# Block-sparse attention and a two-layer FFN: neighbour keys loaded from DRAM instead of copied on chip, and one early load of V put behind the first gathers

## The chip, the cores and the metric

The kernel runs on one core of a Trainium2 chip. The metric is device time in microseconds (us); the profile's span runs from the core's first to its last instruction. Engines are named as the profile does: PE is TensorE (PEld its weight loads), DVE is VectorE, ACT is ScalarE, POOL is GpSimd, SP is SyncE, which here does nothing but issue DMAs.

## The reference

Four batches, eight heads, 768 positions, 64 values a head. Positions are cut into 24 blocks of 32. A query block sees the blocks beside it and itself, the first and the last block, and three sampled blocks; the first and last query block see everything. Behind the softmax and the product with V stands an FFN with softplus between its two matrices.

```python
mask = np.abs(blk_i - blk_j) <= window          # window = 1
mask = mask | (blk_i == 0) | (blk_j == 0) | (blk_i == n_blocks - 1) | (blk_j == n_blocks - 1)
for qb in range(n_blocks):
    for kb in sampled_blocks[qb]:
        mask[qb*block:(qb+1)*block, kb*block:(kb+1)*block] = True
scores = np.where(mask, scores, -1e9)           # then softmax, attn @ v
h = x @ w_in                                    # x: (3072, 512), w_in: (512, 2048)
g = np.maximum(h, 0.0) + np.log1p(np.exp(-np.abs(h)))
return g @ w_out                                # w_out: (2048, 512), float64 weights
```

## The kernel before, in words

**Attention in sets.** The 22 inner query blocks of each of 4 batches make 88 blocks, taken four at a time: 22 groups (`j` from 0 to 21), each one "s" set. A group can straddle two batches (22 is not a multiple of 4): groups 5 and 16 do. The first and last blocks of each batch make four "w" sets, which see all keys. For an "s" set, four query blocks each have eight key blocks: slots 0 to 2 hold the three neighbours, 3 and 7 the first and last block, 4 to 6 the sampled ones. They are laid side by side in one of two key buffers `kg`, which groups use in turn (`kd = kg[j % 2]`, line 504).

**Keys.** A batch's keys lie in SBUF in one tile `kT` (lines 451 to 457), loaded by SP; there is one buffer, so the next batch's load waits for the "w" set's scores, which are the last readers. `gather_keys` (line 503) makes the pieces of work that fill `kg`: `beside` (line 511) copies the three neighbours of all blocks of the group in one VectorE copy (line 515; ScalarE for group 0) and, where the batch changed, the two end blocks (line 524, ScalarE). `of_block` (line 531) copies the sampled blocks, three GpSimd copies a query block (line 544), the block number read from a register. The group's first `of_block` calls `beside`.

**Values.** `load_values` (line 553) fills one of two buffers `vbuf`: the rows of the near blocks in one SP DMA of 1 MB from a host-made array (line 568), the sampled rows by four indirect DMAs of GpSimd, 256 KB each (line 572). "w" sets load whole rows of V (line 563).

**A set's work.** `scores` (line 586; matmuls at 605, mask and minimum by VectorE at 611), `exponents` (ACT, 660), `transposes` (PE 673, copies out of PSUM at 676 and 678), `products` (PE 709), `normalise` (745), `turn` (771), then the high and low parts of x (784, 788). Line 629 holds the "w" sets' scores, 723 their products.

**Order.** SP runs in program order, POOL too in a few stretches; the other engines' order comes from a scheduler, except where an instruction is held in program order. `pieces` (line 795) lists the attention's pieces; `attend` (line 904) issues one, then takes one or two waiting key and value pieces (`gather`, line 481) and then steps of `convert`, the splitting of the float64 weights: raw loads by SP (line 178, four buffers, so each waits for VectorE to be done with an older one), ACT at 185 and 189, VectorE at 195 to 212, parking of later weights by SP (line 231). `scored` asks for the keys of group j + 2 once group j's scores are issued (line 809); `valued` asks for the values two sets ahead. In the program, line 513's work of group j + 2 so stands right behind the load of the queries of set m + 2 (line 468). From some 50 us on, attention is woven with the FFN's first part (hidden layer 263 to 265, projection 327 to 329); behind it the second part runs with PE alone in front (1113 to 1115, 1225 to 1227).

**The start.** SP issues, in this order: keys of batch 0 (line 454), queries of sets 0 and 1 (468), near rows of set 0 and of set 1 (568), queries of set 2 (468), three raw weight loads (178). POOL, in program order: the gathers of set 0 (572), the twelve key copies of group 1 (544):

```python
    load_values(0)
    ...
    with tc.manual_schedule(engines={mybir.EngineType.Pool}):
        gathered(value_work, 0)
        gathered(key_work, 1)
    load_values(1)
```

Of the kernel before, what the change touches and what calls it, by code (L numbers as in the profile page):

```python
# [19 lines left out]
BLOCK = 32  # L20
# [17 lines left out]
PARK = 8  # L38

WARM = 28  # L40

AHEAD = 0.5

# [11 lines left out]
def sparse_attention_ffn(  # L55
# [25 lines left out]
    nc = tc.nc  # L81
    NM, P, NP, NI, _ = q.shape
# [10 lines left out]
    NR = 3  # L93
# [293 lines left out]
    for rows in (slice(0, NR * BLOCK), slice(NR * BLOCK, P)):  # L387
        nc.gpsimd.iota(first[rows], pattern=[[0, 1]], base=0, channel_multiplier=1)
    vbuf = [ac.tile([P, 2, NI, DM], F32, name=f"vg{n}") for n in range(2)]

    nc.gpsimd.indirect_dma_start(
        out=vbuf[0][:, 0, 0, :], out_offset=None, in_=v,
# [55 lines left out]
    kT, qc, vg = {}, {}, {}  # L448
# [23 lines left out]
    def registers(eng, us):  # L472
        for u in us:
            if (eng, u) not in regs:
                regs[eng, u] = eng.value_load(pk32[0:1, u : u + 1], min_val=0, max_val=(1 << 31) - 1)
        return [regs[eng, u] for u in us]
# [9 lines left out]
    def gathered(work, m):  # L486
        while work and work[0][0] <= m:
            work.pop(0)[1]()
# [3 lines left out]
    def load_keys(*js):  # L492

        for j in js:
            if j < NM:
                of = [b for b, _ in group[j]]
                wanted.extend((j, b, of.index(b), of.index(b) + of.count(b)) for b in sorted(set(of)))
        while wanted and wanted[0][1] in kT and not waiting:
            gather_keys(*wanted.pop(0))
# [3 lines left out]
    def gather_keys(j, b, lo, hi):  # L503
        kd = kg[j % 2]
        blk0 = group[j][lo][1]

        stale = [i for i in range(lo, hi) if ended_in.get((j % 2, i)) != b]
        for i in stale:
            ended_in[j % 2, i] = b

        def beside():

            at = kT[b][:, blk0 - 1 : blk0 - 1 + NR, :]
            pattern = [list(x) for x in at.ap]
            ins = (nc.vector.tensor_copy if j else nc.scalar.copy)(
                out=kd[:, lo:hi, 0:NR, :].rearrange("p i s f -> p i (s f)"),
                in_=bass.AP(at.tensor, at.offset, [pattern[0], [NP * BLOCK, hi - lo], [1, NR * NP * BLOCK]]),
            )
            tc.keep_in_program_order(ins)
            if stale:  # L520
                rows = slice(stale[0], stale[-1] + 1)
                first = nc.vector.tensor_copy if j == 0 else nc.scalar.copy
                for end, slot, blkno in ((first, NR, 0), (nc.scalar.copy, 2 * NR + 1, LAST)):
                    ins = end(
                        out=kd[:, rows, slot, :],
                        in_=kT[b][:, blkno : blkno + 1, :].to_broadcast([P, len(stale), NP * BLOCK]),
                    )
                    if j or slot > NR:
                        tc.keep_in_program_order(ins)

        def of_block(i):

            eng = (nc.vector if i < 2 else nc.scalar) if j == 0 else nc.gpsimd
            copy = nc.scalar.copy if j == 0 and i >= 2 else eng.tensor_copy
            if i == lo and j:
                beside()
            blk = group[j][i][1] - 1
            (r,) = registers(eng, [blk // 2])
            for s in range(NR):
                x = nc.s_assert_within(  # L540
                    eng.snap((r >> (16 * (blk % 2) + 5 * s)) & 31), 0, LAST,
                    skip_runtime_bounds_check_because="a sampled block is one of the key blocks",
                )
                copy(  # L544
                    out=kd[:, i, 1 + NR + s, :], in_=kT[b][:, bass.ds(x, 1), :].rearrange("p n f -> p (n f)")
                )

        if j == 0:
            key_work.append((j, beside))
        key_work.extend((j, lambda i=i: of_block(i)) for i in range(lo, hi))  # L550


    def load_values(m):
        if m >= len(sets):
            return
        what, j = sets[m]
        vd = vg[sets[m]] = vbuf[m % 2]
        if what == "w":
            b = j
            rows = vd.rearrange("p c i f -> p (c i) f")  # L560
            for n in range(0, NCH, 2):
                lo = b * S + n * P
                nc.sync.dma_start(
                    out=rows[:, n : n + 2], in_=v[lo : lo + 2 * P].rearrange("(t p) f -> p t f", p=P)
                )
            return
        i0 = 1 if m == 0 else 0
        nc.sync.dma_start(out=vd[:, 0, i0:NI], in_=near[j, :, i0:NI])

        def of_block(i):  # L570
            b, blk_ = group[j][i]
            nc.gpsimd.indirect_dma_start(  # L572
                out=vd[:, 1, i, :],
                out_offset=None,
                in_=v,
                in_offset=bass.IndirectOffsetOnAxis(ap=ix[:, b, blk_ : blk_ + 1], axis=0),
            )

        value_work.extend((m, lambda i=i: of_block(i)) for i in range(NI))
# [288 lines left out]
    warm = ps_s.tile([P, 4, P], F32, tag="s", name="warm")  # L868
    for n in range(WARM):
        nc.tensor.matmul(warm[:, n % 4], ident, ident, start=True, stop=True)  # L870
# [12 lines left out]
    with tc.manual_schedule(engines={mybir.EngineType.Pool}):  # L883
        gathered(value_work, 0)
        gathered(key_work, 1)
    load_values(1)
    load_keys(2)
    scores(1)
# [577 lines left out]
```

## Time and profile before

| | us |
|---|---|
| median of 3 runs | 762.72 (761.26 to 763.01) |
| the profiled execution | 759.56 |
| its span | 757.8 |

| engine | busy us | share |
|---|---|---|
| ACT | 555.1 | 73% |
| POOL | 274.6 | 36% |

HBM reads are 105.97 MB and writes 30.41 MB. In the page's slices each digit is the tenth of a slice (18.9 us) in which an engine was busy. A row of the windows view gives, for one stretch, each engine's busy us (with the count of its instructions), the granted clock of PE, the busy share of the 16 DMA engines and what they moved. A row of the timeline gives start, duration, engine, line and tile, and in brackets how long the engine stood idle ahead of it and who ended that. The chain of waits gives start, duration and what.

### The profile page before, as it was taken

How to read it: one execution, taken by the hardware profiler on the slowest of the kernel's cores; microseconds unless marked ns; L12 is line 12 of the kernel's file. 1: busy time of each engine (PE TensorE's matmuls, PEld its weight loads, DVE VectorE, ACT ScalarE, POOL GpSimd, SP SyncE). 2: the span in 40 equal slices, each digit the busy share in tenths (PEclk: the TensorE clock that was granted, in tenths of full speed). 3: DMA queues.
4: the chain of work that ended last, by engine and by line, in shares of the span. 5: the costliest groups of instructions: out<-in, count | busy, mean ns of one | idle time of the engine just before them, and what ended most of it. 6: DMA issues, size and time to landing. Idle time of an engine off the chain costs nothing.

```text
span 757.8 us, 21892 instructions
## 1 busy us (share of the span) xinstructions
PE 726.4 (96%) x8324; PEld 618.0 (82%) x8324; DVE 587.7 (78%) x1445; ACT 555.1 (73%) x1298; POOL 274.6 (36%) x446
## 2 busy tenths in 40 slices
PE   7888899999999999999999989999999999999997
PEld 5557677878887787887889877899999999999995
DVE  5689999877888779886688775777676776766865
ACT  5679997877878788876678668766676566675663
POOL 7754535415454146540200259551515125020000
PEclk9899999999999999999999999999999999999999
DMA  8788875969658897667526261131133023300301
GB/s 330 259 314 336 336 256 190 348 221 382 244 181 329 281 358 266 229 252 240 196 106 240 100 209 51 62 112 56 58 112 112 25 87 112 106 8 1 112 1 56
DMA packets 54335, 137.79 MB, mean 182 GB/s; under 512 B 5781, under 2 KB 18582, under 8 KB 50518
## 3 DMA queue, kind: packets, MB, share of 16 engines
q1 hardware_dynamic: 46740, 112.40, 41.8%
q0 software_dynamic: 7120, 23.34, 8.3%
q8 instruction: 65, 1.06, 0.6%
q10 hardware_dynamic: 370, 0.66, 0.2%
q14 instruction: 40, 0.33, 0.1%
HBM read 105.97 MB, written 30.41 MB: 180 GB/s over the span
## 4 chain that ended last, share of the span: by engine, by line
PE 69%; ACT 12%; DVE 10%; DMA 4%; issue 3%; POOL 2%; SPq 1%; POOLq 0%; DVEq 0%; ACTq 0%
PE o L1225 7%; PE o L1226 7%; PE o L1227 7%; PE h L263 3%; PE t L673 3%; PE x L709 3%; PE a L1113 3%; PE a L1115 3%; PE a L1114 3%; ACT pr L660 3%; PE h L264 3%; PE h L265 3%; PE o L327 3%; PE o L328 3%; PE o L329 3%; PE s L605 3%
## 5 line engine op out<-in xcount | busy, mean ns | idle before, releaser
L572 POOL DMA_INDIRECT vg<-in_v_dram,ix x88 | 95.6, 1087 | 103.5 <-PE x L709 78.1
L660 ACT ACTIVATE pr<-pr,nmax 128x256 f32<-128x256 f32 (+1 forms) x192 | 102.0, 533 | 30.2 <-DVE nmax L611 20.2
L544 POOL COPY kg<-kT 128x128 f32 x252 | 73.7, 333 | 87.7 <-PE s L605 82.9
L1225 PE MATMUL o<-w,gh 128*128 128x512 f32 x240 | 94.3, 393 | 0.0
L1226 PE MATMUL o<-w,gh 128*128 128x512 f32 x240 | 94.2, 393 | 0.0
L1227 PE MATMUL o<-w,gl 128*128 128x512 f32 x240 | 94.0, 392 | 0.0
L1200 ACT CAST gh<-a 128x512 fp32r<-128x512 f32 x30 | 17.6, 587 | 79.1 <-DVE a L1196 79.1
L263 PE MATMUL h<-x,w 128*128 128x384 f32 x192 | 69.4, 361 | 2.9 <-ACT pt L678 1.3
L611 DVE CUSTOM_DVE_ANT_1 pr<-s,mask 128x256 f32<-128x256 f32 x176 | 62.9, 420 | 7.4 <-PE s L605 7.4
L265 PE MATMUL h<-x,w 128*128 128x384 f32 x192 | 64.8, 338 | 0.1
L264 PE MATMUL h<-x,w 128*128 128x384 f32 x192 | 64.8, 337 | 0.0
L673 PE MATMUL t<-ident,pr 128*128 128x128 f32 x448 | 61.3, 278 | 2.3 <-ACT pr L660 0.9
L709 PEld LDWEIGHTS x<-vg,pt 128*32 128x32 f32 x2816 | 42.1, 110 | 23.6 <-issue 17.7
L327 PE MATMUL o<-w,gh 128*128 128x512 f32 x144 | 58.8, 408 | 0.0
L673 PEld LDWEIGHTS t<-ident,pr 128*128 128x128 f32 x448 | 51.0, 142 | 8.7 <-ACT pr L660 3.5
L709 PE MATMUL x<-vg,pt 128*32 128x64 f32 x2816 | 48.2, 220 | 9.4 <-issue 6.1
L329 PE MATMUL o<-w,gl 128*128 128x512 f32 x144 | 57.1, 397 | 0.0
L328 PE MATMUL o<-w,gh 128*128 128x512 f32 x144 | 57.0, 396 | 0.0
L605 PE MATMUL s<-kg,qc 64*32 64x256 f32 x1408 | 52.2, 391 | 1.8 <-DVE u L276 1.4
L1227 PEld LDWEIGHTS o<-w,gl 128*128 128x128 f32 x240 | 45.1, 188 | 10.1
L1184 DVE SCALAR_TENSOR_TENSOR b<-b,e 128x512 f32<-128x512 f32 x30 | 20.9, 698 | 39.8 <-ACT l L1180 39.8
L678 ACT COPY pt<-t 128x512 f32<-128x512 f32 x82 | 45.8, 585 | 6.9 <-PE t L673 6.8
(207 smaller groups left out, 2147.5 us busy)
## 6 DMA issues: line engine op xcount, KB each, us to landing
vg<-in_near_dram SPq DMA_DIRECT2D x21, 1024.0 KB, 5.7
xD<-x SPq DMA_DIRECT2D x8, 1536.0 KB, 12.7
raw<-in_w_in_dram SPq DMA_DIRECT2D x16, 512.0 KB, 9.0
raw<-in_w_out_dram SPq DMA_DIRECT2D x16, 512.0 KB, 6.8
q<-xD SPq DMA_DIRECT2D x16, 512.0 KB, 7.0
vg<-in_v_dram SPq DMA_DIRECT2D x12, 512.0 KB, 4.5
yD<-os SPq DMA_DIRECT2D x24, 256.0 KB, 3.2
y<-yD SPq DMA_DIRECT2D x24, 256.0 KB, 3.5
```

What stands on the lines that cost most here:

```text
L263: nc.tensor.matmul(out_, wh[:, cols], hi, start=(c == 0), stop=False)
L264: nc.tensor.matmul(out_, wh[:, cols], lo, start=False, stop=False)
L265: nc.tensor.matmul(out_, wl[:, cols], hi, start=False, stop=(c == NC - 1))
L327: nc.tensor.matmul(po[m], gh[:, cols], wh, start=first, stop=False)
L329: nc.tensor.matmul(po[m], gl[:, cols], wh, start=False, stop=last)
L572: nc.gpsimd.indirect_dma_start(out=vd[:, 1, i, :], out_offset=None, in_=v, in_offset=bass.IndirectOffsetOnAxis(ap=ix[:, b, blk_ : blk_ + 1 ...
L660: nc.scalar.activation(x, x, AF.Exp, bias=nmax[:, r, j : j + 1], scale=-1.0, accum_out=rs[:, h : h + 1])
L673: nc.tensor.transpose(ps[:, i], st["pr"][r][:, c * P : (c + 1) * P], ident)
L709: nc.tensor.matmul(xq[rows, h * D : (h + 1) * D], pt[r, 2 * j + c][:, rows], vd[:, c, i, h * D : (h + 1) * D], start=(c == 0), stop=(c == 1),)
L1225: nc.tensor.matmul(po[m], gh[:, cols], wh, start=first, stop=False)
L1226: nc.tensor.matmul(po[m], gh[:, cols], wl, start=False, stop=False)
L1227: nc.tensor.matmul(po[m], gl[:, cols], wh, start=False, stop=last)
```

## The change

From group 4 on (`LOADED = 4`), the three neighbours' keys of a group come in one SP DMA straight from the keys in DRAM, `k[b]`, into `kg`, in place of the VectorE copy out of `kT`. The groups 1 to 3 keep the copy. Shapes and destination are the same: for each partition and query block one run of 3 x 128 float32. The DMA is no longer held in program order with VectorE; SP's own order is the program's. Second, POOL clears one element a partition of `vbuf[1]`'s first near row behind the gathers of set 0 and the key copies of group 1; the near load of set 1 writes over it and so waits for it.

```diff
+LOADED = 4
...
         def beside():
-            at = kT[b][:, blk0 - 1 : blk0 - 1 + NR, :]
+            at = (kT[b] if j < LOADED else k[b])[:, blk0 - 1 : blk0 - 1 + NR, :]
             pattern = [list(x) for x in at.ap]
-            ins = (nc.vector.tensor_copy if j else nc.scalar.copy)(
-                out=kd[:, lo:hi, 0:NR, :].rearrange("p i s f -> p i (s f)"),
-                in_=bass.AP(at.tensor, at.offset, [pattern[0], [NP * BLOCK, hi - lo], [1, NR * NP * BLOCK]]),
-            )
-            tc.keep_in_program_order(ins)
+            out_ = kd[:, lo:hi, 0:NR, :].rearrange("p i s f -> p i (s f)")
+            in_ = bass.AP(at.tensor, at.offset, [pattern[0], [NP * BLOCK, hi - lo], [1, NR * NP * BLOCK]])
+            if j < LOADED:
+                tc.keep_in_program_order((nc.vector.tensor_copy if j else nc.scalar.copy)(out=out_, in_=in_))
+            else:
+                nc.sync.dma_start(out=out_, in_=in_)
...
         gathered(value_work, 0)
         gathered(key_work, 1)
+        nc.gpsimd.memset(vbuf[1][:, 0, 0, 0:1], 0.0)
     load_values(1)
```

## The prediction

> **What bounds the kernel now.** I read the page's busy shares and slices first, then the windows by stage, then the chain and the timeline of the places the change touches.
>
> ```profile
> PE 726.4 (96%) x8324; PEld 618.0 (82%) x8324; DVE 587.7 (78%) x1445; ACT 555.1 (73%) x1298; POOL 274.6 (36%) x446
> ...
> PE   7888899999999999999999989999999999999997
> ...
> DMA  8788875969658897667526261131133023300301
> ```
>
> PE is busy 96% of the span. The holes are in the first five or six slices (0 to 114 us); that is also where the DMA engines are fullest. The windows say what is full there:
>
> ```profile
> 30.00:66.00 36.00, 29.20 (x626) 20.38 (x627) 32.73 (x98) 29.15 (x75) 20.57 (x34) 1.00 0.84 305
> 66.00:124.00 58.00, 53.46 (x933) 42.30 (x932) 57.25 (x158) 53.09 (x142) 33.06 (x69) 1.00 0.82 306
> 124.00:335.00 211.00, 207.04 (x3403) 173.09 (x3403) 175.64 (x495) 173.17 (x450) 93.76 (x193) 1.00 0.75 272
> ```
>
> From 66 to 124 us VectorE is busy 57.25 of 58 us: it is the bound there, ScalarE (53.09) and PE (53.46) next. From 124 us PE is busy 207.04 of 211 us and VectorE only 83%: VectorE time is worth little there. The first 26 us are bound by something else:
>
> ```profile
> 18.07 0.30 PE L709 MATMUL x<-vg,pt 128*32 128x64 f32 x2 [2.24 <-DMA vg<-in_v_dram,ix]
> 19.16 0.42 PE L709 MATMUL x<-vg,pt 128*32 128x64 f32 x2 [0.79 <-DMA vg<-in_v_dram,ix]
> 19.51 1.54 PE L673 MATMUL t<-ident,pr 128*128 128x128 f32 x6
> ...
> 22.59 3.60 PE L605 MATMUL s<-kg,qc 64*32 64x256 f32 x62
> 26.13 1.77 PE L709 MATMUL x<-vg,pt 128*32 128x64 f32 x112
> ```
>
> PE stands 2.24 and 0.79 us for the first set's gathers, and everything behind them queues: transposes, set 1's scores, the rest of set 0's products at 26.13. The chain of waits agrees; its longest piece before 30 us is the last gather:
>
> ```profile
> 9.21 9.91 DMA vg<-in_v_dram,ix
> ```
>
> **Part one: the near load of set 1 goes behind the gathers.**
>
> ```profile
> 3.67 0.95 SPq L568 DMA_DIRECT2D vg<-in_near_dram  x2
> 12.74 0.33 SPq L468 DMA_DIRECT2D qc<-in_q_dram  x1
> 13.12 1.42 SPq L178 DMA_DIRECT2D raw<-in_w_in_dram  x3
> ```
> ```profile
> 0.88 0.10 POOL L375 MEMSET zero<- 128x1 f32 x1
> ...
> 10.19 2.95 POOL L544 COPY kg<-kT 128x128 f32 x12
> 13.56 1.47 POOL L572 DMA_INDIRECT vg<-in_v_dram,ix  x1 [0.41 <-issue]
> ```
> ```profile
> DMA packets 829, 3.20 MB, mean 399 GB/s; under 512 B 99, under 2 KB 99, under 8 KB 822
> ...
> q0 software_dynamic: 163, 0.56, 17.5%
> ```
> ```profile
> q0 software_dynamic: 267, 0.88, 32.0%
> ```
>
> The added clear stands behind POOL's copies, which end at 13.14. POOL's next instruction starts at 13.56, so the clear, 0.10 us like the one at line 375, fits into the 0.41 us that POOL idles, and POOL is not on the chain after 9.21. SP issues the near load at about 13.4 in place of 4.1 and holds the queries of set 2 and three raw loads behind it: 12.74 becomes about 13.8, 13.12 about 14.2, 1 us late. The queries are read by set 2's scores, long after; the raw loads are read by ACT's first conversions, looked at below.
>
> The gain: from 4 to 12 us the DMA engines moved 3.20 MB at 399 GB/s, of which POOL's queue (q0) got 0.56 MB; from 12 to 19.12 it got 0.88 MB (0.124 MB/us) beside SP's queue, which at 12 us was on the 1.05 MB that now come later. The first gathers are five of 128 x 512 float32, 1.31 MB in all, so 0.75 MB are open at 12 us. Alone on the engines they take 0.75 / 0.399 = 1.9 us at best, 6 us as now. The last gather then lands between 14 and 19.1 us. I take 15.5, nearer the fast end, since SP's queue has nothing to move between the first near load and some 15 us.
>
> What is late next?
>
> ```profile
> 20.67 0.58 ACT L678 COPY pt<-t 128x512 f32<-128x512 f32 x1 [3.83 <-PE t L673]
> ...
> 27.14 0.69 ACT L185 ACTIVATE wt<-raw 128x512 f32<-128x512 f32 x1
> ```
> ```profile
> 16.00:19.00 3.00, 0.30 (x2) 0.14 (x2) 1.57 (x4) 0.83 (x4) 2.39 (x3) 1.00 1.03 386
> 19.00:26.00 7.00, 6.84 (x74) 3.33 (x74) 1.37 (x7) 2.01 (x5) 3.00 (x13) 0.51 0.73 280
> ```
> ```profile
> 31.59 2.32 PE L605 MATMUL s<-kg,qc 64*32 64x256 f32 x64
> ```
>
> ACT finished the exponents at 20.67 - 3.83 = 16.84, and the transposes need them: they move from 19.51 to some 16.5, 3 us. Next, the clock: after 3 us in which PE was busy 0.30, the granted clock is 0.51 from 19 to 26, and 62 score matmuls took 3.60 us where 64 took 2.32 at full clock. If the idle stretch goes, that is worth 3.60 - 2.32 = 1.3 us more; if the clock halves anyway, nothing. I take it, since with the gathers there by 15.5 that stretch holds transposes and scores. The products at 26.13 so come 3 to 4.3 us earlier. (The Trainium skill, "TensorE: Matmul & The Clock Gate", part 1, says that the clock halves after at least one idle window of about 3.4 us, free-running. By it the halving could stay if the window happens to lie over what idle time is left; the sum would then lose the 1.3 us, and one run's row cannot decide it.)
>
> Then the first raw load is late:
>
> ```profile
> DMA to landing us min/median/max: 8.2/8.2/8.2
> ```
>
> Issued at 13.12 it landed at 21.3, and ACT wanted it at 27.14. Now it is issued 1 us later and has the whole near load, 1.05 MB, freshly ahead of it on SP's queue where most of that had gone by 15 us: some 2.5 us more at 0.4 MB/us. It lands at about 23.7, while ACT would ask for it at 27.14 - 4.3 = 22.8. ACT waits for it in order, so the gain is cut to 27.14 - 23.7 = 3.4. I take **-3.5 us** (from 0, if the gathers do not speed up, to -6, if both the load and the clock are kind). The work from 26 to 66 us hangs on relative waits, so the shift should last.
>
> **Part two: the neighbours' keys by DMA.**
>
> ```profile
> L515 DVE COPY kg<-kT x23: 542/950/1128, 13.2 to 330.1; 128x1536 f32<-128x1536 f32 x19, 128x768 f32<-128x768 f32 x4
> ```
> ```profile
> 67.03 0.47 DVE kg L515
> ...
> 101.58 0.87 DVE kg L515
> ...
> 118.70 0.87 DVE kg L515
> ...
> 291.17 0.96 DVE kg L515
> ```
>
> Of 23 copies on VectorE three stay, so 16 full ones (0.95) and 4 halves (0.55) go: 17.4 us of VectorE. By stage: one half and four full ones lie in 66 to 124 us (0.55 + 4 x 0.95 = 4.3 us), where VectorE is full. Three of them are on the chain there with 2.2 us. VectorE falls to 53 us, level with ACT and PE, so the most is 4.3 and the least 0. I take **-2.0**, the chain's share. Elsewhere only the copy at 291.17 is on the chain: **-0.5** (0 to -1).
>
> Added: 20 SP DMAs, 16 x 0.786 + 4 x 0.393 = 14.2 MB. Are they in time, and what do they hold up?
>
> ```profile
> 77.04 0.94 DVE L515 COPY kg<-kT 128x1536 f32<-128x1536 f32 x1
> ```
> ```profile
> 94.81 1.96 PE L605 MATMUL s<-kg,qc 64*32 64x256 f32 x42 [0.41 <-issue]
> ```
> ```profile
> 68.16 0.33 SPq L178 DMA_DIRECT2D raw<-in_w_out_dram  x1
> ```
> ```profile
> DMA to landing us min/median/max: 12.4/12.4/12.4
> ```
> ```profile
> 84.44 0.70 ACT L185 ACTIVATE wt<-raw 128x512 f32<-128x512 f32 x1
> ```
>
> Group 6's copy at 77.04 is not read before 94.81: 17 us, while the slowest load quoted here took 12.4. On SP the new load stands right behind the queries of set m + 2, whose buffer waits for the same scores of set m, so SP should not stand longer than now. Behind it are raw weight loads, parks and near loads. The tightest I found is the raw load of 68.16: landed at 80.6, read at 84.44, 3.8 us to spare. One full key load takes 0.786 / 0.373 = 2.1 us of the engines (306 GB/s at 0.82 busy is 373 when full). That hides. I take **+0.5** for traffic (0 to +9, below).
>
> **Sum:** -3.5 - 2.0 - 0.5 + 0.5 = -5.5 us. The profiled execution's 759.56 becomes 754.1; it lies under the median of the runs, 762.72, from which the same sum gives 757.2.
>
> **Rivals.** *The DMA engines become the bound.* From 66 to 124 us they moved 306 x 58 = 17.7 MB; 4.5 key loads add 3.5. The 21.3 MB at 373 GB/s take 57.1 us, so the stage can shrink by 0.9 and not 2, and the start's shift is half lost to the same fullness in 30 to 66 us. Then -2.5 us: 760.2. For it: 0.84 and 0.82 busy. Against it: loads have slack and can run over into the emptier time from 124 us. (The Trainium skill, "DMA: Bandwidth & Descriptors", "Where 436 GB/s comes from", puts loads from HBM at some 358 GB/s; by that the stage would take 59.5 us, and the sum would lose its -2.0 and 1.5 more. The trace disagrees with the limit: 386 and 399 GB/s above.)
>
> *Slower: a weight load runs out of slack.* A raw load behind a key load, queued behind a near load, is late by more than the 3.8 us to spare; then ACT stops in order and all behind it. It decides from two full key loads' delay (4.2 us) on. With six groups before 124 us each losing 2 us, +12 - 5.5 = +6.5: 769.
>
> *The gathers do not speed up,* because POOL's own queue sets their pace: part one is worth 0 and the rest -2.0: 760.7.
>
> *Instruction fetch gets slower,* as it shares the engines:
>
> ```profile
> q8 instruction: 65, 1.06, 0.6%
> ```
> ```profile
> PEld x L709 <- issue: 17.7, 28, 2.5
> ```
>
> PE stood 17.7 us at the products for nothing the profile shows; a tenth more is +1.8: 759.0, inside the forecast's range.
>
> **How the numbers follow.** About 0.3% (2.3 us) is what a measurement can tell from no change. Chances: forecast 0.50, engines full 0.20, gathers no faster 0.15, slower 0.15. The forecast is faster (0.50); the second is half below 760.4 and half within the bound; the third lies at its edge, a third faster: 0.50 + 0.10 + 0.05 = 0.65 faster, 0.20 the same, 0.15 slower. The range: at the low end all kind bounds, -6 - 4.3 - 1 = -11.3, 751.4; at the high end the two quiet rivals with 2 us of late loads, 764.5.
>
> **What would show it.** Right: the near load of set 1 issued near 13.4; last first-set gather landed by 16; no clock of 0.5 before 30 us; set 0's last products by 23; VectorE under 54 us in its stage; 20 new SP DMAs, none of which PE waits for. Wrong: ACT at line 185 or POOL at 544 waiting for DMAs, DMA busy 1.0 through 66 to 124 us, PE's L709 still held at 18 us.

## The result and the profile after

| | before | after |
|---|---|---|
| median, six runs each on one chip, us | 762.97 (761.26 to 763.92) | 768.25 (767.03 to 769.63) |
| profiled execution, us | 759.56 | 767.6 |
| its span, us | 757.8 | 765.5 |

The changed kernel is slower: ratio 1.0061, 95% interval 1.0050 to 1.0073, some 5 us. The prediction said 5.5 us faster. The profiled execution of before lies 3.4 us under the median of its runs, that of after only 0.65 us under its own, so the 8 us between the two profiles overstate the difference.

The page of the changed kernel, busy shares, DMA slices, all DMA and the instruction queue:

```profile
PE 732.3 (96%) x8324; PEld 624.6 (82%) x8324; DVE 573.7 (75%) x1425; ACT 556.6 (73%) x1298; POOL 265.8 (35%) x447
...
DMA  8799986869888999879616460230233023200301
...
DMA packets 63871, 151.95 MB, mean 199 GB/s; under 512 B 6101, under 2 KB 28118, under 8 KB 60054
...
q8 instruction: 65, 1.06, 0.5%
```

VectorE has 14 us less to do, as meant, and PE has 5.9 us more busy time for the same 8324 matmuls: more of them ran at a lower clock. The windows of the changed kernel, the stretches of the prediction (columns: PE, PEld, DVE, ACT, POOL, granted clock, DMA share, GB/s):

```profile
16.00:19.00 3.00, 2.79 (x28) 1.22 (x27) 2.25 (x10) 2.21 (x9) 2.39 (x3) 1.00 1.02 392
19.00:26.00 7.00, 6.12 (x184) 3.76 (x182) 5.13 (x21) 5.55 (x17) 4.77 (x16) 1.00 1.02 387
30.00:66.00 36.00, 29.54 (x563) 20.63 (x548) 26.75 (x86) 24.21 (x64) 16.55 (x30) 0.91 0.82 289
66.00:124.00 58.00, 50.01 (x898) 40.88 (x899) 52.45 (x150) 51.55 (x138) 29.97 (x67) 0.94 0.86 322
124.00:335.00 211.00, 206.42 (x3369) 171.74 (x3371) 162.93 (x467) 169.71 (x434) 84.96 (x184) 1.00 0.87 317
```

The first two rows are what was hoped for: the clock is 1.00 from 19 to 26 us, where it was 0.51 before. From 66 to 124 us VectorE has its slack (52.45 of 58), but PE is busy 50.01 instead of 53.46 us: nobody uses the slack. The start itself, timeline of the changed kernel on PE, then on SP, then on POOL:

```profile
16.29 0.43 PE L712 MATMUL x<-vg,pt 128*32 128x64 f32 x16
...
19.05 3.48 PE L608 MATMUL s<-kg,qc 64*32 64x256 f32 x62
22.46 1.77 PE L712 MATMUL x<-vg,pt 128*32 128x64 f32 x112
```
```profile
3.73 10.60 SPq L571 DMA_DIRECT2D vg<-in_near_dram  x2
14.46 1.04 SPq L470 DMA_DIRECT2D qc<-in_q_dram  x1
15.54 1.38 SPq L180 DMA_DIRECT2D raw<-in_w_in_dram  x3
```
```profile
13.87 0.10 POOL L889 MEMSET vg<- 128x1 f32 x1
```

PE no longer waits for a gather (no bracket at 16.29), and the rest of set 0's products starts at 22.46 instead of 26.13: 3.67 us ahead. By the fourth score set all of it is gone: it starts at 41.6 us, before it was 40.6. The waits list of the changed kernel says where PE stands:

```profile
PEld x L712 <- issue: 22.0, 36, 3.3
```

This was 17.7 us: PE stands at the products longer "for nothing that the profile shows". The longest of these stops, timeline of the changed kernel on PE, and then the same place before:

```profile
84.96 1.25 PE L608 MATMUL s<-kg,qc 64*32 64x256 f32 x32
86.14 1.70 PE L712 MATMUL x<-vg,pt 128*32 128x64 f32 x105
91.04 0.31 PE L712 MATMUL x<-vg,pt 128*32 128x64 f32 x5 [3.20 <-issue]
...
92.42 0.52 PE L267 MATMUL h<-x,w 128*128 128x384 f32 x1
```
```profile
85.22 1.77 PE L709 MATMUL x<-vg,pt 128*32 128x64 f32 x112
87.56 0.31 PE L709 MATMUL x<-vg,pt 128*32 128x64 f32 x6 [0.57 <-issue]
```

PE breaks off inside one set's products, just before their end, for 3.20 us instead of 0.57; the hidden layer's matmuls behind it take 0.52 us where 0.34 is usual. The window says why they do, granted clock 0.50 for 3.4 us:

```profile
92.10:95.50 3.40, 3.40 (x13) 3.31 (x13) 2.62 (x6) 0.42 (x2) 2.79 (x3) 0.50 1.02 385
```

**What PE waits for there.** The instruction queue q8 moved 65 packets, 1.06 MB, 16 KB each. PE left 8324 matmuls, 8324 weight loads and, among them, its semaphore waits: 16,820 records before, that is 65 times 256 and a rest, and at 64 bytes an instruction 256 of them are 16 KB. I read this as q8 bringing PE's program in blocks of 256 instructions. Counted through the trace in order of time, semaphore waits included (without them the borders do not line up), the product at 91.04 is PE's record 2753 = 10 x 256 + 193. In the two kernels and the twelve experiments PE stands for over 1 us inside the products of the "s" sets, between 24 and 420 us, 34 times, and 33 of these stand at 193 or 194 in their 256 (the one other is told at the end): the border of a block. The DMA view, cut to windows, shows when that block's packet ran (q1 is SP's queue, q0 GpSimd's). The changed kernel, 85.1 to 88.4 us and then 88.4 to 89.6:

```profile
q1 hardware_dynamic: 670, 1.22, 101.5%
q0 software_dynamic: 25, 0.05, 3.9%
...
q1 hardware_dynamic: 143, 0.46, 97.8%
q8 instruction: 1, 0.02, 5.8%
```

The kernel before, 84.4 to 85.2 us and then 85.2 to 86.3:

```profile
q1 hardware_dynamic: 77, 0.27, 86.8%
q0 software_dynamic: 4, 0.00, 1.6%
...
q1 hardware_dynamic: 38, 0.11, 26.0%
q8 instruction: 1, 0.02, 5.7%
```

PE crossed the border ahead of this one at 84.45 us before and at 85.16 after. If that is when the next block is asked for, its packet started 0.76 us later before, when SP's queue (q1) was running dry, and 3.30 us later after, behind 670 packets of q1 that kept the engines full. The packet takes 1.0 to 1.1 us, and PE goes on 1.2 to 1.6 us after its end. PE's 256 instructions here, nearly all small products, last only 2.4 us. So before: 0.76 + 1.00 + 1.35 - 2.35 = 0.76 us of stop; after: 3.30 + 1.10 + 1.48 - 2.44 = 3.44 (from start to start of the products 0.79 and 3.42 are measured; the timeline's idle is 0.2 us less). This sum divides up the measured stop; what it shows is that the packet's wait is the term that grew. The Trainium skill, "Runtime: NRT & Kernel Launch", "Instruction fetch mechanics", tells of the 16 KiB blocks, fetched ahead by a DMA queue of the engine's own, and calls the cost of a border mostly hidden. The traces agree with the block and differ on the cost.

That full engines go with a late packet holds at all borders. In the fourteen traces, between 20 and 420 us, 609 packets start over 0.1 us behind their crossing. Where the other queues kept the 16 engines under 20% busy (from 0.5 us ahead of the crossing to 1.0 behind it; 141 borders) the median wait is 0.76 us; where they kept them 95% busy or more (310 borders) it is 2.41 us.

### The profile page after: what moved, and what is told of

Read it like the earlier page. It is cut to its first block, busy times and chain, and to the rows that moved or that the text cites. A ratio compares the mean times of both kernels' runs of the same rounds, so it can differ in the third digit from the quotient of the medians.

```text
span 765.5 us, 21910 instructions
## 1 busy us (share of the span) xinstructions
PE 732.3 (96%) x8324; PEld 624.6 (82%) x8324; DVE 573.7 (75%) x1425; ACT 556.6 (73%) x1298; POOL 265.8 (35%) x447
## 3 DMA queue, kind: packets, MB, share of 16 engines
q8 instruction: 65, 1.06, 0.5%
## 4 chain that ended last, share of the span: by engine, by line
PE 72%; ACT 12%; DVE 9%; issue 4%; POOL 1%; DMA 1%; DVEq 0%; SPq 0%; POOLq 0%; ACTq 0%
PE o L1229 7%; PE o L1230 7%; PE o L1231 7%; PE x L712 5%; PE t L676 4%; ACT pr L663 4%; PE s L608 4%; PE h L265 3%; PE a L1117 3%; PE a L1119 3%; PE a L1118 3%; PE o L329 3%; PE h L266 3%; PE h L267 3%; PE o L330 3%
## 5 line engine op out<-in xcount | busy, mean ns | idle before, releaser
L575 POOL DMA_INDIRECT vg<-in_v_dram,ix x88 | 89.5, 1017 | 108.7 <-PE x L712 83.8
L547 POOL COPY kg<-kT 128x128 f32 x252 | 71.1, 326 | 99.1 <-PE s L608 91.4
L1204 ACT CAST gh<-a 128x512 fp32r<-128x512 f32 x30 | 17.6, 588 | 79.1 <-DVE a L1200 79.1
L712 PEld LDWEIGHTS x<-vg,pt 128*32 128x32 f32 x2816 | 45.2, 114 | 24.1 <-issue 22.0
L712 PE MATMUL x<-vg,pt 128*32 128x64 f32 x2816 | 51.7, 227 | 9.4 <-issue 9.4
L278 DVE SCALAR_TENSOR_TENSOR u<-h,e 128x384 f32<-128x384 f32 x48 | 26.6, 555 | 33.4 <-ACT e L272 29.7
```

The lines of the kernel that those rows point to most:

```text
L575: nc.gpsimd.indirect_dma_start(out=vd[:, 1, i, :], out_offset=None, in_=v, in_offset=bass.IndirectOffsetOnAxis(ap=ix[:, b, blk_ : blk_ + 1 ...
L712: nc.tensor.matmul(xq[rows, h * D : (h + 1) * D], pt[r, 2 * j + c][:, rows], vd[:, c, i, h * D : (h + 1) * D], start=(c == 0), stop=(c == 1),)
```

## The experiments

Stops are given from start to start, for the border at record 2753 ("the stop at 88 us"), unless another is named. Ratios are to the kernel before on the same chip; its medians were 763.28, 761.04 and 763.94 us in the three sets of four experiments.

Theories: (1) instruction fetch: loads keep the DMA engines full while a block is fetched, PE stops at its border, and a long stop halves the clock; (2) bytes: the engines are simply fuller and everything is a little late, in proportion to the volume; (3) order: without the copies the scheduler orders PE, VectorE and ScalarE otherwise, and that costs.

### The change taken apart

**memset_only**: the clear at line 889 alone, `LOADED = 99`.

> The change's second part alone: the near load of set 1 waits for the first gathers, all neighbour keys are still copied by VectorE. Every engine's order is that of the kernel before but for the one clear on GpSimd. The changed kernel's profile has set 0's last products at 22.46 us in place of 26.13. Traffic theory and order theory alike: that gain lasts, -3 to -4 us. Start theory (the earlier start is what brings the new stops of PE at lines 712 from 31 to 35 us, and the halved clock behind them): 0 to +3 us, with the stops at 31 us there.

760.66 us, ratio 0.9975 (0.9950 to 1.0000). The clear alone gains some 2 us, at the edge of what can be told and short of the 3 to 4 that were expected; set 0's last products start at 22.06, as early as with the whole change, but a half clock of 3.4 us follows from 26.95 us on. The stops at 31 us, which the start theory expected, are not there.

**keys_only**: the loads alone.

```diff
-        nc.gpsimd.memset(vbuf[1][:, 0, 0, 0:1], 0.0)
```

> The change's first part alone: neighbour keys of groups 4 to 21 by SyncE's DMAs, the near load of set 1 as before. Traffic theory and order theory: the whole loss is here and the start's gain is missing, +7 to +9 us against the kernel before. Start theory: -2 to -3 us, as VectorE's 17 us are gone.

768.70 us, ratio 1.0070 (1.0045 to 1.0095): with the loads the clear is worth 0.1%, less than can be told.

**no_keys**: as keys_only, but the neighbours' keys of the groups from 4 on are neither copied nor loaded; their scores use what lies in `kg`. The order of instructions on PE, VectorE, ScalarE and GpSimd is that of keys_only.

```diff
             else:
-                nc.sync.dma_start(out=out_, in_=in_)
+                pass
```

> Groups 4 to 21 get no neighbour keys at all, neither copied nor loaded (their scores use what groups 2 and 3 left there). The order on PE, VectorE, ScalarE and GpSimd is exactly that of the first part alone; only the 20 DMAs of 14.2 MB are missing. Traffic theory (the fuller DMA engines make PE's instruction fetch and loads late): -2 to -4 us, VectorE's relief without its price. Order theory (without the copies the scheduler lines up VectorE's weight splitting ahead of the attention's work, and that is what stops PE): +6 to +9 us, as with the DMAs.

762.95 us, ratio 0.9993 (0.9973 to 1.0013). Relief of VectorE and new order come to nothing together. So (3) is not the loss, and the -2.5 us that the prediction put on VectorE's relief are not there (this run cannot tell whether the order eats a gain of that size).

**traffic_only**: all copies stay, in the order of before, and SP issues the twenty loads at their places into a DRAM buffer that nothing reads (so they write to HBM too, which the change does not).

```diff
+            tc.keep_in_program_order((nc.vector.tensor_copy if j else nc.scalar.copy)(out=out_, in_=in_))
+            if j >= LOADED:
+                wide = [[list(x) for x in src.ap][0], [NP * BLOCK, hi - lo], [1, NR * NP * BLOCK]]
+                nc.sync.dma_start(out=idle[:, 0 : hi - lo], in_=bass.AP(src.tensor, src.offset, wide))
```

> All neighbour keys are copied by VectorE as before, and the same 20 loads of 14.2 MB are issued by SyncE at the same places, but into DRAM that nobody reads. The order on PE, VectorE, ScalarE and GpSimd is exactly that of the kernel before. Traffic theory: +5 to +9 us, with longer stops at PE's products. Order theory: 0 to +1 us.

768.63 us, ratio 1.0065 (1.0040 to 1.0091): the whole loss of the change, without any of its edits to the computation. The stop at 88 us, timeline on PE:

```profile
94.28 0.31 PE L712 MATMUL x<-vg,pt 128*32 128x64 f32 x6 [3.65 <-issue]
94.52 0.56 PE L265 MATMUL h<-x,w 128*128 128x384 f32 x1
```

**Where keys_only loses against no_keys.** These two have one order and differ in the loads alone. Their score sets start together until 83 us; keys_only is then late by 1.5 us (at the start of the next score set), 3.0 (at 134.6), 4.4 (at 186.5), 5.2 (at 231.7) and 5.5 (at 277.1), and stays there: its span is 5.3 us longer. Timeline of keys_only on PE at the first three steps, then of no_keys at the same instructions:

```profile
92.22 0.31 PE L712 MATMUL x<-vg,pt 128*32 128x64 f32 x5 [3.44 <-issue]
...
120.36 3.31 PE L712 MATMUL x<-vg,pt 128*32 128x64 f32 x128
...
157.53 0.38 PE L676 MATMUL t<-ident,pr 128*128 128x128 f32 x2 [1.78 <-ACT pr L663]
```
```profile
90.75 0.31 PE L712 MATMUL x<-vg,pt 128*32 128x64 f32 x4 [2.03 <-issue]
...
118.91 1.99 PE L712 MATMUL x<-vg,pt 128*32 128x64 f32 x128
...
153.57 0.33 PE L266 MATMUL h<-x,w 128*128 128x384 f32 x1 [0.42 <-issue]
```

The first step is the stop at 88 us, 1.4 us longer. The second is a half clock: 128 products take 3.31 instead of 1.99 us, and the matmuls behind them 0.3 more. Ahead of it both kernels stand equally long, 2.34 and 2.35 us, for VectorE, at no border; only keys_only's clock halves. So these 1.5 us are no late fetch; the part on why the prediction was wrong tells what they hang on. The third is another block border: the view names ScalarE, but the record is 4801 = 18 x 256 + 193, its packet ran from 154.99 to 156.06 us, and PE goes on 1.47 us after that, as at the other borders; in traffic_only, where the same record is a hidden-layer matmul that waits for no exponent, PE stops there for 1.79 us too. Three small stops at borders, at 205, 220 and 235 us, make up the rest (0.6, 0.2 and 0.3 us). Borders so hold some 3.8 of the 5.3 us and the half clock 1.5; waits for the twenty key loads come to 0.4 us on PE and 0.5 us on VectorE in all.

### Which loads

**early5** and **late15**: traffic_only with the first five loads alone (3.15 MB, issued from 40 to 90 us), and with the last fifteen alone.

```diff
-            if j >= LOADED:
+            if LOADED <= j < 8:
```
```diff
-            if j >= LOADED:
+            if j >= 8:
```

> All copies are kept as in the kernel before, and only the first five of the twenty extra loads are issued (into memory that nothing reads; those that SyncE issues between 39 and 89 us): a quarter of the bytes of traffic_only. Theory of the instruction fetch (the loss is the late fetch of one block of TensorE's instructions at about 88 us, and the half clock after it, and these five loads are the ones in its way): most of traffic_only's loss stays, 766.5 to 768.5 us, the stop at about 90 us is over 3 us long and a half clock follows it. Rival, bytes (the loss grows with the volume that the engines carry): a quarter of 5.3 us, 764.6 us. Rival, a raw weight load out of slack: a stop at a weight step (L184) in place of that in the products.

764.33 us, ratio 1.0042 (1.0020 to 1.0063).

> All copies are kept, and only the last fifteen of the twenty extra loads are issued (from about 104 us on), three quarters of the bytes of traffic_only. Theory of the instruction fetch: the stop at 87 us is as in the kernel before (at most 1.8 us, no half clock after it), and the time is 763.3 to 764.8 us. Rival, bytes: three quarters of 5.3 us, 767.3 us.

762.74 us, ratio 1.0022 (1.0002 to 1.0041). The timeline on PE at the stop, early5 and then late15:

```profile
92.19 0.31 PE L712 MATMUL x<-vg,pt 128*32 128x64 f32 x6 [3.08 <-issue]
```
```profile
90.68 0.31 PE L712 MATMUL x<-vg,pt 128*32 128x64 f32 x6 [0.60 <-issue]
```

The two losses add up to the whole. The five early loads, 22% of the bytes, make about two thirds of it, and late15 has the stop of the kernel before; volume alone would have split them the other way. The forecasts in us were made from a kernel before at 763.28; on this chip it takes 761.04. As they were written, early5's 764.33 is the bytes rival's 764.6, and late15's 762.74 lies under both forecasts. As differences to before, early5's +3.3 us stands at the low end of theory (1)'s +3.2 to +5.2 (bytes: +1.3), and late15's +1.7 just above theory (1)'s 0 to +1.5 (bytes: +4.0): I had put nearly all of the loss at this one border, and some of it is elsewhere.

**one_load** and **four_loads**: of the five early loads only the fourth, and the other four.

```diff
+            loads.extend([j] if j >= LOADED else [])
-            if j >= LOADED:
+            if j >= LOADED and len(loads) == 4:
```

> All copies are kept, and one of the twenty extra loads alone is issued, the fourth (0.79 MB of 14.2, issued at about 78 us), into memory that nothing reads. Theory of the instruction fetch (this load's packets keep the DMA engines full while the block that TensorE needs at about 88 us is asked for): the stop at 88 us is 3 us or longer, a half clock of 3.4 us follows it, and the time is 2 to 4 us above the kernel before. Rival, bytes: 0.79 of 14.2 MB of 5.3 us, 0.3 us above it, with the stop as before (at most 1.8 us).

766.24 us, ratio 1.0038 (1.0021 to 1.0055): 0.79 MB cost 2.9 us, ten times their share of the bytes. The stop is 2.46 us, 1.7 longer than before but shorter than forecast, and the clock stays at 1.00; where the rest of the 2.9 us is lost I did not place:

```profile
92.69 0.31 PE L713 MATMUL x<-vg,pt 128*32 128x64 f32 x6 [2.24 <-issue]
```

> All copies are kept, and of the first five extra loads the other four are issued (2.36 MB; about 40, 51, 65 and 90 us). Theory of the instruction fetch at 88 us: the stop there is at most 1.8 us without a half clock, and the time is at most 1 us above the kernel before. Rival, bytes: 2.36 of 14.2 MB of 5.3 us, 0.9 us. Rival, another block (the one that TensorE needs at about 47 us is held by the first two loads): about 2 us above the kernel before, with the stop at 47 us over 3 us and a half clock behind it.

764.95 us, ratio 1.0023 (1.0011 to 1.0036), nearer the third expectation than the first two, though the stop at 47 us is not over 3 us. Timeline on PE, the border at 47 us and the one at 88:

```profile
49.72 0.54 PE L713 MATMUL x<-vg,pt 128*32 128x64 f32 x24 [2.24 <-issue]
...
92.08 0.31 PE L713 MATMUL x<-vg,pt 128*32 128x64 f32 x6 [1.53 <-issue]
```

Here the stop at 88 us stays short, and PE is stopped at 47 us, with a half clock behind it (50.9 to 54.3 us). Before, the stop at 47 us was as long, 2.57 us from start to start, without the half clock.

### Moving the border, moving the load

**shift**: the changed kernel, with 64 fewer PE instructions ahead of the work, so that each border falls 64 instructions later in it.

```diff
-    for n in range(WARM):
-        nc.tensor.matmul(warm[:, n % 4], ident, ident, start=True, stop=True)
+    for n in (4, 4, 4, 4, 4, 2, 1, 1, 1, 1, 1, 1):
+        nc.tensor.matmul(warm[:, 0:n], ident, ident[:, None, :].to_broadcast([P, n, P]), start=True, stop=True)
```

> The changed kernel with the 28 warm-up products at its start written as 12 of the same 3584 columns: TensorE's program is 64 instructions shorter ahead of all else, and every border of a 16 KB instruction block falls 64 instructions later in the work; loads, copies and their order are those of the changed kernel. Theory of the instruction fetch: the stop of 3.4 us at 87.6 us and the half clock after it go, the seventh score set starts at most 14.5 us after the sixth (17.5 us in the changed kernel), a stop stays or appears near 47 us, and smaller ones may appear between 195 and 260 us, where borders then fall beside the start of short stretches; 763 to 767 us. Rival, a load that lands late or engines that are simply full: the stop stays at the same products, 17.5 us between these score sets, 768 us.

Timeline of shift on PE, the same products, the place where the border now falls, and the next score set:

```profile
79.12 1.76 PE L712 MATMUL x<-vg,pt 128*32 128x64 f32 x110
80.82 0.44 PE L265 MATMUL h<-x,w 128*128 128x384 f32 x1
...
85.06 0.60 PE L774 MATMUL y<-ident,xs 128*128 128x128 f32 x4
...
89.70 2.03 PE L608 MATMUL s<-kg,qc 64*32 64x256 f32 x64 [1.16 <-issue]
```

All loads are there, the engines are as full (the windows give 391 GB/s from 76 to 92 us), and 110 products run through without a stop; the next score set starts 14.4 us after the last one instead of 17.6, at full clock. (The 1.16 us ahead of it are no border's: it is record 2847, 31 in its 256, and PE stands in a semaphore wait there from 88.16 to 89.65.) The packet for the border at 85.06 still came 2.64 us behind the crossing ahead (79.22); but the block in between now holds hidden-layer matmuls and lasts 5.8 us instead of 2.4, and that covers the fetch. That is the fetch theory's, and against the others. The time is not: 765.33 us, ratio 1.0080 (1.0050 to 1.0110), as slow as the changed kernel. The stops moved with the borders: start to start 2.96 us at 240.6 us and 2.56 at 299.4, where the changed kernel has 0.64 and none at the same work. The ten runs spread from 762.52 to 772.65; the profiled one is the lowest. A shift picks other places to stop at, not fewer.

**one_copy**: the changed kernel with its fourth load (issued at 76.7 us) made VectorE's copy again.

```diff
+            loads.append(j) if j >= LOADED else None
+            copied = j < LOADED or len(loads) == 4
```

> The changed kernel with the fourth of its twenty loads (issued at 76.7 us) made VectorE's copy again; the other nineteen and the memset stay. Theory of the instruction fetch: the stop at 88 us falls from 3.4 us to at most 1.8 us, the half clock behind it goes, and the ratio to the kernel before falls from 1.006 to 1.000 to 1.002. Rival, bytes: 18/19 of the loss stays, ratio 1.0055 to 1.006.

767.36 us, ratio 1.0052 (1.0032 to 1.0072), and the stop hardly shrinks:

```profile
90.80 0.43 PE L714 MATMUL x<-vg,pt 128*32 128x64 f32 x5 [2.89 <-issue]
```

Theory (1) as I stated it here, one load in the way of one block, is wrong. The border ahead was crossed at 85.15 us and the packet ran at 88.29, without that load. no_keys shows the other part: with no key load at all it waits 2.43 us and stops for 2.25. From the issue of that set's near load to the border ahead there are 10.2 us in the kernel before, 9.3 in no_keys and one_copy: in the order without copies PE arrives sooner behind the same burst of V, query and weight loads, and may so meet its tail; that is argued, not shown. With the new order (no_keys) or with the one load (one_load) the packet is late at this border. Each is one profiled execution, though, and memset_only, with neither, waits 1.78 us too: a difference of 1 us between two of these waits is no proof of a cause. What the order does there it gives back elsewhere, since no_keys loses nothing in all.

**loaded8** and **loaded8_no_memset**: `LOADED = 8`, with and without the clear.

```diff
-LOADED = 4
+LOADED = 8
```

> The changed kernel with LOADED = 8 in place of 4: the first five loads are VectorE's copies again, the other fifteen stay loads, and the memset stays. Theory of the instruction fetch: the stop at 88 us is at most 1.8 us, and the time is that of the memset alone, 760 to 762 us. Rival, bytes: memset's time plus three quarters of the traffic's 5.3 us, 764.7 us.

> LOADED = 8 without the memset; order and loads are those of loaded8. If the memset is worth here what it was worth alone (0.25%), the ratio to the kernel before is 0.998 (0.996 to 1.000). If loaded8's gain came from VectorE's relief after 90 us, it stays at 0.9955.

757.60 us, ratio 0.9954 (0.9933 to 0.9974), and 763.65 us, ratio 0.9999 (0.9982 to 1.0015). The stop at 88 us in loaded8:

```profile
85.42 0.31 PE L712 MATMUL x<-vg,pt 128*32 128x64 f32 x6 [0.58 <-issue]
```

loaded8 beats both kernels (3.4 us under before; as a difference, theory (1) forecast 1.3 to 3.3 under it, bytes 1.4 over it). Its gain is the clear's: without it nothing is left, and the fifteen late loads, with what they take off VectorE, are neither gain nor loss. Whether it beats memset_only (0.9975) the intervals leave open.

The fetch of one block, from the instruction records and q8's packets, one profiled execution each (us; "order" says whether the engines' order is that of before or the one without copies):

| kernel | border ahead crossed | packet starts | wait | order | stop |
|---|---|---|---|---|---|
| before | 84.45 | 85.21 | 0.76 | before | 0.79 |
| late15 | 87.55 | 88.32 | 0.78 | before | 0.82 |
| four_loads | 88.01 | 89.68 | 1.67 | before | 1.75 |
| memset_only | 84.95 | 86.72 | 1.78 | before | 1.75 |
| one_load | 87.91 | 90.33 | 2.42 | before | 2.46 |
| early5 | 86.58 | 89.95 | 3.38 | before | 3.30 |
| traffic_only | 88.09 | 91.84 | 3.75 | before | 3.87 |
| no_keys | 86.00 | 88.44 | 2.43 | new | 2.25 |
| one_copy | 85.15 | 88.29 | 3.14 | new | 3.11 |
| after | 85.16 | 88.46 | 3.30 | new | 3.42 |
| keys_only | 86.11 | 89.83 | 3.71 | new | 3.65 |

The stop follows the packet's wait almost one to one; while the packet waited, the engines moved 389 to 410 GB/s in the five rows with a wait over 3 us, and 337 and 317 in before and late15.

## Why the prediction was wrong

**The start** was right in its mechanism and size: near load issued about 14.0 (13.4 forecast), gathers in time for products at 16.29, no half clock before 30 us, products at 22.46 (by 23). Wrong was "the shift should last". Between 28.0 and 41.6 us the changed kernel stops five times for about 0.75 us and then runs 6.8 us at half clock:

```profile
31.47 0.23 PE L712 MATMUL x<-vg,pt 128*32 128x64 f32 x1 [0.33 <-issue]
32.21 0.22 PE L712 MATMUL x<-vg,pt 128*32 128x64 f32 x1 [0.51 <-issue]
32.96 0.22 PE L712 MATMUL x<-vg,pt 128*32 128x64 f32 x1 [0.54 <-issue]
```

These stops are no border's (records 913 to 923); one_copy has four of the kind at the same place, the last 1.43 us long, and the last is the exception named above. They begin while a block is being fetched, and what paces them I could not settle. PE was busy only 1.39 of the 3.41 us ahead of the half clock. Measured, the clear is worth 0.25% alone, 0.45% in loaded8 and 0.1% with all loads.

**VectorE's relief** (-2.0 and -0.5): VectorE did fall under 54 us in its stage, and together with the new order it bought nothing (no_keys 0.9993). The chain of waits went through its copies, but PE, ScalarE and VectorE were near one another there (53 to 57 of 58 us), and the new order brought PE to a block border sooner.

**Traffic** is the step that failed: "That hides. I take **+0.5** for traffic". It measured +0.65% (traffic_only) or +5.7 us (keys_only against no_keys). The term's own bound, 0 to +9, held this, but the high end of the range took 2 us of it. I looked for who would read the loads late, and at that the prediction held: in the waits list ScalarE never waits at 187 for a raw load, POOL waits at 547 for a batch's keys no longer than before (3.0 us, 3.5 before), PE waited 0.8 us in all for the twenty loads, and "engines full" (DMA 1.0 through 66 to 124 us) did not come, 0.86. The rival "Slower" named 769, near the measured 768.25, but that is luck: its mechanism, ScalarE stopping for a raw load, did not occur. The harm went to a customer that no semaphore shows. The instruction fetch stood among the rivals, with the right mechanism and the wrong price: "a tenth more" of the 17.7 us of stops. But the cost of a border is no share of a sum: it is the queue's wait at one moment, at this border 0.8 us when the engines run dry and 1.7 to 3.8 when they are full, and at 88 us the kernel before happened to come just as the queue ran dry. On top comes the clock, which the rival left out: 3.4 us at half speed, some 1.7 us of work.

**Why some stops bring a half clock and others of the same length do not** can be read from the traces. In each of them the clock changes only at steps of 3.413 us: the changed kernel's half clocks start at 34.04, 92.07 and 119.37 us, 17 and 8 such steps apart. From 24 to 420 us the clock falls to a half 23 times in the fourteen traces, each time behind a step in which PE was busy 44% or less, and it never falls behind one with 45% or more. So a stop of 2 to 2.5 us can halve the clock where it lies inside one step, and need not where it lies across two. The second loss of keys_only against no_keys is a close case; keys_only first, the step with the stop and the one behind it:

```profile
117.37:120.78 3.41, 1.44 (x59) 0.99 (x63) 3.38 (x9) 2.83 (x8) 0.28 (x2) 1.00 0.27 109
120.80:124.20 3.40, 3.40 (x114) 3.23 (x103) 3.40 (x17) 3.40 (x13) 3.37 (x11) 0.50 0.03 5
```
```profile
116.01:119.42 3.41, 1.53 (x66) 1.08 (x70) 3.38 (x11) 2.83 (x8) 0.37 (x2) 1.00 0.00 0
119.40:122.80 3.40, 3.40 (x123) 3.27 (x112) 3.40 (x17) 3.40 (x13) 3.37 (x11) 1.00 0.30 53
```

PE was busy 42% and 45% of them. Where the steps fall relative to the work is nothing that the change chose, so in this pair of executions the 1.5 us are chance of where the stop lay.

**What stays open:** the 0.75 us stops at 31 us; and how gains and losses combine. Measured one by one, clear, order and loads (-0.25%, -0.07%, +0.65%) make +0.33% and not +0.61%; one_load and four_loads make +0.61% and their union early5 +0.42%.

## What to carry to other kernels

Price added DMA traffic not only by who reads it, but by what else crosses those engines: a stretch of many small instructions uses up a 16 KB block of PE's program in 2.4 us, less than the next block's fetch takes (0.8 + 1.0 + 1.4 = 3.2 us when the engines run dry, up to 6.2 behind a full queue). Count the instruction records to find the borders, look whether the queue is empty when one is crossed, and put bulk loads where PE's instructions are long; here five loads up to 90 us cost 0.4%, and the fifteen behind them 0.2%. Taking copies off an engine on the chain bought nothing measurable here, where two others were nearly as full.

## What the runs showed of the hardware

- PE's program comes in 65 packets of 16 KB, a block of 256 records each, and data on the other queues holds them up. At the border at 88 us the packet started 0.7 to 0.8 us after PE crossed the border ahead when the engines ran dry, and up to 3.75 us after it when they moved 380 to 410 GB/s (medians over all borders: 0.76 and 2.41 us). At every border where PE stood for over 1 us, it went on 1.2 to 1.6 us after the packet's end.
- The granted clock changed only at steps of 3.413 us, and fell to a half behind the steps in which PE was busy 44% or less, between 24 and 420 us in fourteen traces. The Trainium skill, "TensorE: Matmul & The Clock Gate", part 1, puts the half clock behind an idle window of about 3.4 us, free-running. The traces agree with the window; in no_keys the one ahead of the half clock (88.7 to 92.1 us) held a stop of 2.03 us and work for the rest, so here less than a whole window's idleness was enough.
